# Batch 0 of a linear-attention and MLP kernel: nine tokens to a partition, and 64x64 products in place of 128x128 ones

## The chip, the core and the metric

The kernel runs on one core of a Trainium2 chip. The metric is the device time of one execution in microseconds (us). The engines of the core are TensorE (PE in the profile, its weight loads PEld), VectorE (DVE), ScalarE (ACT), GpSimd (POOL) and SyncE (SP). Each works through its own queue in program order and waits there for semaphores. GpSimd, SyncE and ScalarE also issue DMA transfers.

## What is computed

Eight batches of linear attention with eight heads, 576 tokens and a head size of 64 are followed by a two-layer MLP with a residual. Cut to what matters:

```python
q_s = softmax(q, axis=-1)                 # over the 64 columns of a head
k_s = softmax(k, axis=2)                  # over the 576 tokens
kv  = einsum('bhsd,bhse->bhde', k_s, v)   # 64x64 per head
x   = einsum('bhsd,bhde->bhse', q_s, kv)  # then heads side by side: (8, 576, 512)
xn  = (x - mean(x)) / sqrt(var(x) + 1e-6) * g_ln
out = x + maximum(xn @ w_ch1, 0) @ w_ch2  # 512 -> 2048 -> 512
```

All inputs and the output are float32. The kernel computes in bfloat16 with float32 accumulation.

## The kernel before

The tokens are worked off in chunks: chunk c from 0 to 7 is the first 512 tokens of batch c, as four tiles of 128 tokens, and chunk 8 holds the last 64 tokens of all eight batches. While TensorE runs the MLP of one chunk, the attention of the next chunks is done beside it. `run` (line 849) walks the list of the MLP's products and puts each side job ahead of the product at which its due number is reached. The program order on every engine is thus written out by hand.

Batch 0 has no earlier MLP to lie beside. It is done in `first_batch` (lines 957 to 1053), and this is what the change rewrites. Its steps are:

- **Loads.** SP issues q's first two tiles (line 978) and then k in four pieces of two heads (line 980). POOL waits for q by copying a few of its elements (`gate`, line 1004), and then issues v in three pieces (line 1006, four, two and two heads, cast to bfloat16 by the DMA), q's last two tiles (line 970), the first 512 columns of w1 in two pieces (line 1013, rows 0 to 255 and 256 to 511), the rest of w1, w2, and the loads of batches 1 and 2 (`load_behind`, line 1067).
- **Layout.** k and v of batch 0 have six tokens of a head in one partition (`T0 = 6`), so that 576 tokens fill 96 partitions.
- **Warm products.** `warm` (line 863) runs products of zeros on TensorE while the data is on its way.
- **q.** `exp_qt` (ScalarE), `norm_q` (VectorE: sum, reciprocal, product) and `eq_pT` (transposes on TensorE, copied out) for tiles 0 and 1.
- **k and v.** For each pair of heads j: `exp_k0` (line 293), the column sums `z0_mm` (line 306, six products with a column of ones), and `kv0_mm` (line 321, six products of 128 columns). The 128x128 result of a pair has the two heads' 64x64 blocks on its diagonal. VectorE takes it out times the reciprocal sum and times a block mask `diag` (line 322), straight into `kv_sb`, and sums each row. ScalarE (line 327) or, for the last pair, VectorE (line 331) spreads the row sum, times -1/512, over 128 columns (`mbc`).
- **x, transposed.** `xT_mm` (line 342) forms x less its mean for tiles 0 and 1, already transposed: one product with `kv_sb` and products with `mbc`, which subtract the mean. `xT_out` takes it out times g.
- **q, tiles 2 and 3.** `exp_qt` and `eq_pT` for them lie among the x products; their x is made later by `q0_rest` (lines 940 and 414), beside the first MLP products.

The first layer of chunk 0 (`mm1_part`, line 520) starts with w1's rows 0 to 255 for four output blocks, and then goes to rows 256 to 511. The two calls of `q0_rest` lie among the first eight of its products. Batch 1's k-v products (`kv_pairs`, line 371) come near the end of chunk 0; they need v of batch 1 (cast by VectorE, line 146) and the exponentials of k's last 64 tokens (line 198). Later batches form x by 64x64 products in two banks (`po_block`, line 403).

Of the kernel before, what the change touches and what calls it, by code (L numbers as in the profile page):

```python
# [20 lines left out]
def kernel(  # L21
# [34 lines left out]
    T0 = 6  # L56
    P0 = S // T0
# [18 lines left out]
    junk = const.tile([P, 256], BF16)  # L76
# [211 lines left out]

    def exp_k0(j):
        hs = slice(2 * j, 2 * j + 2)  # L290
        if j == 0:
            eks[0] = raw.tile([P, T0, H, D], BF16, tag="kt", name="ek0", bufs=1)
        nc.scalar.activation(
            eks[0][0:P0, :, hs, :].rearrange("p t h d -> p h t d"), raws[0][0][0:P0, hs], AF.Exp
        )

    def k0_mm(j, t):
        hs = slice(2 * j, 2 * j + 2)
        return eks[0][0:P0, t, hs, :], raws["v0"][0:P0, hs, t, :], P

    def z0_mm(j):

        if j == 0:
            kvbox["z0"] = mm_ps.tile([P, NP], FP32, tag="m", name="z0")
        for t in range(T0):
            nc.tensor.matmul(
                kvbox["z0"][:, j : j + 1], k0_mm(j, t)[0], ones[0:P0],
                start=(j == 0 and t == 0), stop=(t == T0 - 1), skip_group_check=True,
            )
# [6 lines left out]
    def kv0_mm(j):  # L316
        pool, tag = (att_ps, "a") if j < 2 else (mm_ps, "m")
        pkv = pool.tile([P, P], FP32, tag=tag, name="pkv")
        for t in range(T0):
            lhsT, rhs, w = k0_mm(j, t)  # L320
            nc.tensor.matmul(pkv[:, 0:w], lhsT, rhs, start=(t == 0), stop=(t == T0 - 1))
        nc.vector.scalar_tensor_tensor(
            kv_sb[:, 0, j, :], in0=pkv, scalar=kvbox["rz"][:, j : j + 1], in1=diag,
            op0=ALU.mult, op1=ALU.mult, accum_out=kvbox["sum"][:, j : j + 1],
        )
        if j < NP - 1:
            nc.scalar.activation(
                mbc[:, j], ones_w, AF.Copy, scale=kvbox["sum"][:, j : j + 1]
            )
        else:  # L330
            nc.vector.tensor_scalar_mul(
                out=mbc[:, j], in0=ones_w, scalar1=kvbox["sum"][:, j : j + 1]
            )

    def xT_mm(j, kh):
# [3 lines left out]
        ops = [(kv_sb[:, 0, j, :], j % 2)] if j // 2 == kh else []  # L339
        ops += [(mbc[:, j], i) for i in range(2)]  # L340
        for n, (lhsT, i) in enumerate(ops):
            nc.tensor.matmul(
                pobox["T", kh][:, i], lhsT, eqTs[0][:, 0:2, j, :],
                start=(j == 0 and n == 0), stop=(j == NP - 1 and n >= len(ops) - 2),
                skip_group_check=True,
            )

    def xT_out(i):
        dst, src = xnTs[0][:, 0:2, i, :], pobox["T", i // 2][:, i % 2]
        if i < 2:  # L350
# [3 lines left out]

    halves = (slice(0, 64), slice(64, P))
# [507 lines left out]
    def warm(n, width=256):  # L863

        w = mm_ps.tile([P, 512], FP32, tag="m", name="warm")
        for _ in range(n):
            nc.tensor.matmul(w[:, 0:width], junk[:, 0:P], junk[:, 0:width], start=True, stop=True)
# [83 lines left out]
    def g_columns():  # L951
        gcp = mm_ps.tile([P, KO1], FP32, tag="m", name="gcp")
        nc.tensor.matmul(gcp, raws["g"], ident_f, start=True, stop=True)
        nc.vector.tensor_copy(out=g_one, in_=gcp)
        nc.vector.tensor_scalar_mul(out=g_col, in0=gcp, scalar1=1.0 / DM)

    def first_batch():
# [3 lines left out]
            mlp.tile([P, H, T0, D], FP32, tag="hT", name="kt0", bufs=1), None,  # L961
# [3 lines left out]
        v0 = mlp.tile([P, H, T0, D], BF16, tag="hs", name="v0", bufs=1)  # L965
# [9 lines left out]
        def src0(x, h0, hn):  # L975
            return x[0, h0 : h0 + hn].rearrange("h (p t) d -> p h (t d)", t=T0)

        load_q0(0, 2, nc.sync)
        for h0 in range(0, H, 2):
            nc.sync.dma_start(  # L980
                k0[0:P0, h0 : h0 + 2].rearrange("p h t d -> p h (t d)"), src0(k, h0, 2)
            )
# [10 lines left out]
        nc.vector.memset(ones_w, -1.0 / DM)  # L993
        nc.vector.memset(diag, 0.0)
        for ps in halves:
            nc.vector.memset(diag[ps, ps], 1.0)
        nc.vector.memset(kv_sb[:, 1:B], 0.0)
# [7 lines left out]
        for h0, hn in ((0, 4), (4, 2), (6, 2)):  # L1005
            nc.gpsimd.dma_start(  # L1006
                v0[0:P0, h0 : h0 + hn].rearrange("p h t d -> p h (t d)"), src0(v, h0, hn)
            )
# [12 lines left out]
        warm(34)  # L1021
# [28 lines left out]
        eq_pT(0, 3, nc.vector)  # L1050
        xT_mm(3, 1)
        xT_out(2)
        xT_out(3)

# [136 lines left out]
```

## Time and profile before

| | us |
|---|---|
| median of 3 runs | 263.01 |
| lowest and highest | 262.71 and 263.16 |
| the profiled execution | 262.68 |
| its span, first to last instruction | 260.9 |
| TensorE busy in the span | 254.9 (98%) |
| VectorE busy | 223.3 (86%) |
| ScalarE busy | 177.8 (68%) |
| GpSimd busy | 103.4 (40%) |
| last k exponential of batch 0 ends | 10.29 |
| first k-v product of batch 0 starts | 10.56 |
| first MLP product starts | 15.24 |
| second piece of w1 lands | 17.04 |

The last four rows are positions in the span, counted from its start. A line of a timeline has the start in us, the duration in us, the engine, the line of the kernel, the operation, what it writes and reads, shapes, and the count of instructions merged in it; a bracket at the end gives the idle time of the engine just before and what ended it. The durations of merged products include the time that the last one takes to come out of the array (about 0.2 us), so the starts, not the durations, tell the rate. The granted TensorE clock is 0.997 over the span.

### The profile page before, as it was taken

The numbers are of one execution on the slowest core, as the hardware profiler recorded it, in microseconds if no ns is written. First come the engines' busy times: TensorE is split into PE (matmuls) and PEld (weight loads), VectorE is DVE, ScalarE is ACT, GpSimd is POOL, SyncE is SP. The second block draws the span as 40 slices with busy tenths as digits, with TensorE's granted clock in tenths as the row PEclk, the third lists the DMA queues.
The fourth block names the chain that finished last, engine by engine and source line by source line (L and its number), as shares of the span: only waits on it lengthen the run. The fifth ranks groups of instructions, "written<-read, shape, count | busy, mean of one in ns | idle before, by whom it ended". The sixth has DMA issues, their size and how long they took to land.

```text
span 260.9 us, 7328 instructions
## 1 busy us (share of the span) xinstructions
PE 254.9 (98%) x2904; PEld 218.6 (84%) x2907; DVE 223.3 (86%) x542; ACT 177.8 (68%) x348; POOL 103.4 (40%) x160
## 2 busy tenths in 40 slices
PE   8999999999999999999999999999999999999993
PEld 5889855788888888888888888888888888888883
DVE  6778996989998998899889988998899889957873
ACT  4657790997987785788578857885788386638400
POOL 3953138230199409800890098009100910190000
PEclk9999999999999999999999999999999999999998
DMA  6999999998899996998889968998902630322014
GB/s 190 255 206 206 352 221 274 275 213 273 151 121 314 272 110 139 293 242 88 119 287 259 95 133 290 244 96 166 276 1 45 140 143 4 72 72 101 3 40 121
DMA packets 82618, 45.04 MB, mean 173 GB/s; under 512 B 58196, under 2 KB 79192, under 8 KB 82584
## 3 DMA queue, kind: packets, MB, share of 16 engines
q0 software_dynamic: 32464, 21.76, 44.9%
q1 hardware_dynamic: 49488, 22.29, 37.0%
q10 hardware_dynamic: 632, 0.53, 0.7%
q8 instruction: 22, 0.36, 0.6%
q14 instruction: 12, 0.10, 0.1%
HBM read 36.70 MB, written 9.44 MB: 177 GB/s over the span
## 4 chain that ended last, share of the span: by engine, by line
PE 92%; DMA 4%; POOL 2%; issue 0%; DVE 0%
PE ba L604 21%; PE bx L762 20%; PE bb L762 10%; PE ph L520 8%; PE bb L604 6%; PE be L604 5%; PE bc L604 5%; PE pc L556 5%; PE bc L762 5%; DMA w_raw<-in_moe_w_ch_dram 3%; PE pkv L371 2%; DMA qt<-in_q_dram 2%; PE po L403 2%; PE ptr L928 1%; PE po L414 1%; POOL v L1006 1%
## 5 line engine op out<-in xcount | busy, mean ns | idle before, releaser
L604 PEld LDWEIGHTS <-hs 128*128 128x128 bf16 x512 | 49.6, 98 | 6.0
L269 POOL TENSOR_TENSOR tq<-xnT 128x256 bf16<-128x256 bf16 x30 | 20.1, 671 | 85.5 <-PE bc L604 59.9
L762 PEld LDWEIGHTS <-w_raw 128*128 128x128 bf16 x480 | 46.6, 98 | 5.8 <-DVE bb L793 0.2
L604 PEld LDWEIGHTS <-hT 128*128 128x128 bf16 x392 | 37.6, 98 | 4.2
L762 PEld LDWEIGHTS <-w1g 128*128 128x128 bf16 x360 | 34.7, 98 | 4.3 <-issue 0.2
L762 PE MATMUL bx<-tq,w_raw 128*128 128x256 bf16 x240 | 31.5, 273 | 0.0
L604 PE MATMUL ba<-w_q,hs 128*128 128x256 bf16 x256 | 30.6, 273 | 0.0
L786 ACT COPY bc<-bx 128x512 f32<-128x512 f32 x30 | 16.7, 594 | 19.1 <-PE bx L762 19.1
L427 ACT ACTIVATE scrap<-x,mv 128x512 bf16<-128x512 bf16 x32 | 23.1, 723 | 4.6 <-DVE mv L457 4.4
L793 DVE TENSOR_TENSOR bb<-bx,s 128x512 f32<-128x512 f32 x30 | 19.5, 694 | 7.8 <-ACT s L790 5.1
L804 ACT ACTIVATE hT<-bb 128x512 bf16<-128x512 f32 x30 | 16.3, 594 | 9.5 <-PE bb L762 9.5
L804 ACT ACTIVATE hT<-bc 128x512 bf16<-128x512 f32 x30 | 16.4, 595 | 8.5 <-PE bc L762 8.5
L796 DVE TENSOR_TENSOR hT<-bx,s 128x512 bf16<-128x512 f32 x30 | 19.3, 684 | 2.9 <-PE bx L762 2.7
L587 DVE TENSOR_TENSOR hs<-hT 128x1024 bf16<-128x1024 bf16 x32 | 21.3, 672 | 0.5 <-ACT hT L804 0.5
L229 DVE TENSOR_REDUCE zq<-eq 128x16 f32<-128x1024 bf16 (+1 forms) x20 | 20.7, 1048 | 0.5 <-ACT eq L220 0.5
L269 POOL TENSOR_TENSOR tq<-xnT,tq 128x256 bf16<-128x256 bf16 x30 | 20.0, 669 | 1.1
L449 DVE SCALAR_TENSOR_TENSOR x<-po,rq 128x256 bf16<-128x256 f32 x48 | 17.5, 420 | 1.6 <-PE po L403 1.6
L790 ACT COPY s<-bb 128x512 f32<-128x512 f32 x30 | 16.5, 620 | 0.0
L804 ACT ACTIVATE hT<-bx 128x512 bf16<-128x512 f32 x30 | 16.4, 608 | 0.0
L762 PE MATMUL bx<-xnT,w1g 128*128 128x256 bf16 x120 | 16.2, 273 | 0.0
L762 PE MATMUL bx<-tq,w1g 128*128 128x256 bf16 x120 | 15.9, 272 | 0.0
L762 PE MATMUL bc<-xnT,w1g 128*128 128x256 bf16 x120 | 15.8, 273 | 0.0
(157 smaller groups left out, 539.3 us busy)
## 6 DMA issues: line engine op xcount, KB each, us to landing
out_dram<-ot POOLq DMA_DIRECT2D x30, 256.0 KB, 5.0
kt<-in_k_dram SPq DMA_DIRECT2D x5, 1024.0 KB, 12.5
qt<-in_q_dram SPq DMA_DIRECT2D x4, 1024.0 KB, 8.7
qt<-in_q_dram POOLq DMA_DIRECT2D x2, 1024.0 KB, 12.9
kt<-in_k_dram POOLq DMA_DIRECT2D x2, 1024.0 KB, 14.7
vm<-in_v_dram POOLq DMA_DIRECT2D x16, 128.0 KB, 12.5
qt<-in_q_dram SPq DMA_DIRECT2D x3, 512.0 KB, 7.2
w_raw<-in_moe_w_ch_dram POOLq DMA_DIRECT2D x3, 512.0 KB, 10.8
```

Of the source, the lines that this page charges most:

```text
L229: nc.vector.reduce_sum(eqs[c][1][:, ts], eqs[c][0][:, ts], axis=AX.X)
L269: nc.gpsimd.tensor_tensor(out=dst[:, t], in0=x[:, t], in1=y[:, t], op=ALU.subtract)
L427: nc.scalar.activation(scrap, x[:, t], AF.Square, bias=mv[:, t, 0:1], scale=-float(DM), accum_out=mv[:, t, 1:2],)
L449: nc.vector.scalar_tensor_tensor(x[:, t].rearrange("p (i two d) -> p i two d", two=2, d=D)[:, :, half], in0=pobox[c, t][half], scalar=1.0, ...
L520: nc.tensor.matmul(ph[:, m % 2, at : at + tn], (w1g if c else w1_sb)[:, ko, m * P : (m + 1) * P], xnTs[c][:, t0 : t0 + tn, ko, :], start=( ...
L587: nc.vector.tensor_tensor(out=dst, in0=x, in1=y, op=op)
L604: nc.tensor.matmul(hbox[bank][:, t, cs], lhsT, rhs[:, cs], start=first and (own or t == 0) and k == 0, stop=k == KH - 1, skip_group_check= ...
L762: nc.tensor.matmul(dst[:, q], lhsT, rhs, start=first and q == 0 and ko == 0, stop=ko == 1, skip_group_check=True)
L786: nc.scalar.copy(at[g, "c"], at[g, "x"])
L793: nc.vector.tensor_tensor(out=at[g, "b"], in0=at[g, "x"], in1=at[g, "s"], op=ALU.add)
L796: nc.vector.tensor_tensor(out=h_out(g, 1, 1), in0=at[g, "x"], in1=at[g, "s"], op=ALU.add)
L804: nc.scalar.activation(h_out(g, odd, half), at[g, name], AF.Relu)
```

## The change

Five things change, nearly all in `first_batch` and its helpers:

1. `T0` goes from 6 to 9. A pair of heads then fills all 128 partitions, one head in each half (64 partitions of nine tokens). k still comes in four loads, and v now in four loads of one pair each in place of three.
2. The k-v and z products become 64x64 quarter products, one for each half: 18 per pair in place of six, both halves into one bank. The result of a pair is 128 partitions by 64 columns without the zero blocks, and goes to a new tile `kvc`. The block mask and its memsets go; `kv_sb` is filled from `kvc` by ScalarE copies (`kv0_copy`).
3. The row sum is scaled into one column (`kvm`) by VectorE, and the mean products read that column spread by a step of zero. `mbc` goes. The products of x with k-v become two quarter products per pair.
4. The order is rewritten: x is accumulated for both halves of its columns as each pair comes, warm products between the transposes go from 11 of 256 columns to two of 512, the leading 34 of 256 become 17 of 512, g's columns are copied by ScalarE, and `xT_out` and the last transposes are dealt differently to VectorE and ScalarE. The exponential of q's fourth tile moves behind `xT_out(1)`.
5. In `load_behind`, k's last 64 tokens are loaded ahead of v for batches 1 and 2.

```diff
-    T0 = 6
-    P0 = S // T0
+    T0 = 9
...
-    ones_w = const.tile([P, P], BF16)
-    diag = const.tile([P, P], FP32)
-    mbc = const.tile([P, NP, P], BF16)
+    ones_f = const.tile([P, D], FP32)
+    kvc = const.tile([P, NP, D], BF16)
+    kvm = const.tile([P, NP], BF16)
...
+            eks[0] = raw.tile([P, NP, T0, D], BF16, tag="kt", name="ek0", bufs=1)
+        nc.scalar.activation(eks[0][:, j], raws[0][0][:, j], AF.Exp)
...
         for t in range(T0):
-            nc.tensor.matmul(
-                kvbox["z0"][:, j : j + 1], k0_mm(j, t)[0], ones[0:P0],
-                start=(j == 0 and t == 0), stop=(t == T0 - 1), skip_group_check=True,
-            )
+            for ps in halves:
+                nc.tensor.matmul(
+                    kvbox["z0"][ps, j : j + 1], eks[0][ps, j, t], ones[ps],
+                    start=(j == 0 and t == 0), stop=(t == T0 - 1), skip_group_check=True,
+                )
...
     def kv0_mm(j):
-        pool, tag = (att_ps, "a") if j < 2 else (mm_ps, "m")
-        pkv = pool.tile([P, P], FP32, tag=tag, name="pkv")
+        pkv = att_ps.tile([P, D], FP32, tag="a", name="pkv")
         for t in range(T0):
-            lhsT, rhs, w = k0_mm(j, t)
-            nc.tensor.matmul(pkv[:, 0:w], lhsT, rhs, start=(t == 0), stop=(t == T0 - 1))
+            for ps in halves:
+                nc.tensor.matmul(
+                    pkv[ps], eks[0][ps, j, t], raws["v0"][ps, j, t],
+                    start=(t == 0), stop=(t == T0 - 1), skip_group_check=True,
+                )
         nc.vector.scalar_tensor_tensor(
-            kv_sb[:, 0, j, :], in0=pkv, scalar=kvbox["rz"][:, j : j + 1], in1=diag,
+            kvc[:, j], in0=pkv, scalar=kvbox["rz"][:, j : j + 1], in1=ones_f,
             op0=ALU.mult, op1=ALU.mult, accum_out=kvbox["sum"][:, j : j + 1],
         )
...
+        nc.vector.tensor_scalar_mul(
+            out=kvm[:, j : j + 1], in0=kvbox["sum"][:, j : j + 1], scalar1=-1.0 / DM
+        )
+
+    def kv0_copy(js):
+        for ps in halves:
+            nc.scalar.copy(kv_sb[ps, 0, js, ps], kvc[ps, js])
+
+    def xT_mean(j, kh):
...
+        for i in range(2):
             nc.tensor.matmul(
-                pobox["T", kh][:, i], lhsT, eqTs[0][:, 0:2, j, :],
-                start=(j == 0 and n == 0), stop=(j == NP - 1 and n >= len(ops) - 2),
+                pobox["T", kh][:, i], kvm[:, j : j + 1].to_broadcast([P, P]),
+                eqTs[0][:, 0:2, j, :], start=(j == 0 and i == 0), stop=(j == NP - 1),
                 skip_group_check=True,
             )
+    def xT_kv(j):
+        kh, i = divmod(j, 2)
+        for ps in halves:
+            nc.tensor.matmul(
+                pobox["T", kh][ps, i], kvc[ps, j], eqTs[0][ps, 0:2, j, :],
+                start=False, stop=False, skip_group_check=True,
+            )
...
     def xT_out(i):
-        if i < 2:
+        if i % 2 == 0:
             nc.vector.tensor_scalar_mul(out=dst, in0=src, scalar1=g_one[:, i : i + 1])
...
+    def g_copies():
+        nc.scalar.copy(g_one, raws["gcp"])
+        nc.scalar.activation(g_col, raws["gcp"], AF.Copy, scale=1.0 / DM)
...
+        def src0(x, j):
+            return x[0, 2 * j : 2 * j + 2].rearrange("two (s t) d -> (two s) (t d)", t=T0)
...
+        for j in range(NP):
+            nc.gpsimd.dma_start(v0[:, j].rearrange("p t d -> p (t d)"), src0(v, j))
...
-        nc.vector.memset(kv_sb[:, 1:B], 0.0)
+        nc.vector.memset(ones_f, 1.0)
+        nc.vector.memset(kv_sb, 0.0)
...
-        warm(34)
+        warm(17)
         for t in range(2):
             exp_qt(0, t)
             norm_q(0, t)
         eq_pT(0, 0, nc.vector)
-        warm(11)
-        eq_pT(0, 1, nc.vector)
         for j in range(NP):
             exp_k0(j)
-            z0_mm(j)
-            if j == NP - 2:
-                g_columns()
+        z0_mm(0)
+        g_columns()
+        z0_mm(1)
+        warm(2)
+        eq_pT(0, 1, nc.vector)
+        z0_mm(2)
+        z0_mm(3)
+        g_copies()
         recip_z()
         kv0_mm(0)
         kv0_mm(1)
+        kv0_copy(slice(0, 2))
+        def xT(j):
+            xT_mean(j, 0)
+            xT_mean(j, 1)
+            xT_kv(j)
+        xT(0)
         kv0_mm(2)
-        xT_mm(0, 0)
+        xT(1)
         kv0_mm(3)
         exp_qt(0, 2)
-        exp_qt(0, 3)
-        xT_mm(1, 0)
-        xT_mm(2, 0)
-        xT_mm(0, 1)
-        xT_mm(3, 0)
+        xT(2)
+        kv0_copy(slice(2, 4))
+        xT_mean(3, 0)
         xT_out(0)
         xT_out(1)
-        eq_pT(0, 2, nc.scalar)
-        xT_mm(1, 1)
-        xT_mm(2, 1)
-        eq_pT(0, 3, nc.vector)
-        xT_mm(3, 1)
+        eq_pT(0, 2, nc.vector)
+        exp_qt(0, 3)
+        xT_mean(3, 1)
+        xT_kv(3)
         xT_out(2)
         xT_out(3)
+        eq_pT(0, 3, nc.vector)
...
             if which == 1:
+                load_krem(nc.gpsimd, b)
                 load_v(b)
-                load_krem(nc.gpsimd, b)
```

More of the change, by code (lines that the diff above doesn't have):

```diff
@@ L861, in run, with warm @@
             fn()
-    def warm(n, width=256):
-        w = mm_ps.tile([P, 512], FP32, tag="m", name="warm")
+    def warm(n):
+        w = mm_ps.tile([P, 4, P], FP32, tag="m", name="warm")
         for _ in range(n):
-            nc.tensor.matmul(w[:, 0:width], junk[:, 0:P], junk[:, 0:width], start=True, stop=True)
+            nc.tensor.matmul(w, junk, junk[:, 0:4].to_broadcast([P, 4, P]), start=True, stop=True)
     def prep_fast(b):
@@ L951, in g_columns @@
     def g_columns():
[L952 to L955, printed above, removed]
+        raws["gcp"] = mm_ps.tile([P, KO1], FP32, tag="m", name="gcp")
+        nc.tensor.matmul(raws["gcp"], raws["g"], ident_f, start=True, stop=True)
+    def g_copies():
+        nc.scalar.copy(g_one, raws["gcp"])
+        nc.scalar.activation(g_col, raws["gcp"], AF.Copy, scale=1.0 / DM)
     def first_batch():
@@ L964, in first_batch @@
         k0, _, q0 = raws[0]
[L965 removed]
+        v0 = mlp.tile([P, NP, T0, D], BF16, tag="hs", name="v0", bufs=1)
         raws["v0"] = v0
```

42 lines of the change are left out of this document (5 added, 37 removed).

## The prediction

> **What bounds the kernel now.** I read the windows by stage first. From 45 us to 250 us TensorE is busy without a gap (40.00 of 40.00 us in the line below), and its steps stand in one written order; so whatever comes late or early before 45 us is handed on to the end in full.
>
> ```profile
> 60.00:100.00 40.00, 40.00 (x460) 35.04 (x458) 37.52 (x89) 32.36 (x65) 19.49 (x28) 1.00 1.12 214
> ```
>
> The columns are: stretch, PE, PEld, DVE, ACT and POOL busy, granted clock, DMA share, GB/s. Next the chain that ended last, in order of time: it comes over the second piece of w1 (line 1013, rows 256 to 511 of 512 columns), which lands at 17.04, and from there it is TensorE.
>
> ```profile
> 9.86 7.18 DMA w_raw<-in_moe_w_ch_dram
> 17.04 0.05 issue
> 17.09 0.61 PE ph L520 x4
> ```
>
> Then the timeline of the prologue. The group at 17.09 is the first that needs w1's second piece.
>
> ```profile
> 7.46 0.40 PE L928 MATMUL ptr<-ident,eq 128*128 128x128 bf16 x4
> 10.56 1.25 PE L321 MATMUL pkv<-v,ek 96*128 96x128 bf16 x18
> 11.09 0.35 DVE L322 SCALAR_TENSOR_TENSOR kv_sb<-pkv,rzk,diag 128x128 bf16<-128x128 f32 x1 [0.22 <-PE pkv L321]
> 13.70 0.39 PE L342 MATMUL pxT<-eqT,mbc 128*128 128x256 bf16 x2 [0.26 <-DVE mbc L331]
> 15.24 0.60 PE L520 MATMUL ph<-xnT,w_raw 128*128 128x256 bf16 x4
> 16.55 0.38 PE L414 MATMUL po<-kv_sb,eqT 128*128 128x128 bf16 x4
> 17.09 0.61 PE L520 MATMUL ph<-xnT,w_raw 128*128 128x256 bf16 x4 [0.16 <-DMA w_raw<-in_moe_w_ch_dram]
> ```
>
> The last four products before 17.09 start at 16.55 and follow each other by 0.055, so TensorE alone would have gone on at 16.77. That is 1.53 us after the MLP's first product (15.24), and only 0.32 us ahead of w1. Two paths are level here, loads and TensorE, and the change works on both: the time moves by the later of the two, less 17.09.
>
> **The loads.** In the one-us windows, 4 to 5 moves q (128 partitions) at 390 GB/s and 5 to 8 moves k (96 partitions) at 267 to 269:
>
> ```profile
> 4.00:5.00 1.00, 1.00 (x7) 0.71 (x5) 0.88 (x1) 0.00 (x0) 0.00 (x0) 1.00 1.12 390
> 7.00:8.00 1.00, 1.00 (x13) 0.80 (x11) 1.00 (x2) 0.75 (x2) 1.00 (x2) 1.00 1.09 268
> ```
>
> k is 1.18 MB: 4.4 us at 268, 3.0 at 390. If 128 partitions bring k to q's rate, all that stands behind it (DMA share above 1 in every window from 3 us) comes 1.4 us sooner, and w1's second piece lands at 15.6. Against that POOL issues four v loads for three. The three took 2.13 us, and those of 192 rows 0.65 to 0.67; a fourth puts w1's issue 0.5 to 0.67 later. If landing followed issue alone that is 17.7 at worst. Issue ends near 10.6 now, and the bytes ahead of it move until about 12.6, so I take 15.8. The exponential of a k pair, 0.84 us for 768 columns and 0.575 for q's 512, is 0.64 for 576. The last now ends at 10.29; it would end near 8.9, or 10.06 if k lands as now (9.42).
>
> **TensorE's price of a quarter product.** No row has two 64x64 products side by side. The nearest are the pair products of later batches (128x64, two side by side) and the x products (64x64, four side by side):
>
> ```profile
> 56.71 1.04 PE L762 MATMUL bb<-tq,w_raw 128*128 128x256 bf16 x8
> 57.68 0.32 PE L371 MATMUL pkv<-vm,ek 128*64 128x65 bf16 x8
> ...
> 58.30 0.20 PE L371 MATMUL pkv<-vr,ekr 128*64 128x65 bf16 x2
> 58.44 1.05 PE L762 MATMUL bx<-tq,w_raw 128*128 128x256 bf16 x8
> ```
>
> ```profile
> 91.05 0.49 PE L604 MATMUL ba<-w_sb,hT 128*128 128x256 bf16 x3
> 91.47 0.74 PE L403 MATMUL po<-kv_sb,eqT 64*64 64x64 bf16 x64
> 92.14 0.83 PE L604 MATMUL bb<-w_q,hs 128*128 128x256 bf16 x6
> ```
>
> Forty take 57.68 to 58.30, 16 ns each; 64 take 0.74 less the 0.19 of the last one, 8.7 ns each. I take 16, since two lie side by side in the change as well, for z0's one-column products too (bounds 8.7 and, one after the other, 32). Both blocks also show the price of changing over: full products follow each other by 0.109, so the line 371 block could have begun at 57.59 and began at 57.68 (0.09 in); its last starts at 58.30 and the next full one at 58.44 (0.12 out). Line 403 gives 0.09 and 0.11. The first line 371 block, at 42.22, was left in 0.34. I take 0.09 in and 0.12 out; 0.34 is the upper end, and nothing the lower.
>
> **The sum, up to the first pair product.** The transposes at 7.46 wait for VectorE as now and take 0.22: 7.68. z0(0): 0.09 + 18 x 0.016 + 0.12 = 0.50. g_columns: 0.24 (its two pieces stood 0.12 apart). z0(1): 0.50. warm(2): two of 512 columns, by the 0.216 spacing of line 556's, 0.43. That is 9.35, past the 9.02 at which the second transposes could go (norm_q ends at 8.96), so 0.33 us of that wait's cover is overdrawn. Transposes 0.22, into quarters 0.09, z0(2) and z0(3) 0.58: T = 10.24 for the first k-v product, against 10.56. v's first pair, the first of four, should have landed (the four-head load now lands near 10.5). The 34 warm products become 17 of twice the width: nothing. The 11 removed took 1.2 us, spent waiting for norm_q anyway.
>
> **From T to the MLP.** Now 15.24 - 10.56 = 4.68. After: the first VectorE take-out at T + 0.48 (18 x 0.016, the 0.17 that lay between last product and 11.09, a little for the handover). 64 columns for 128 save 0.07 of 0.35; its accumulator read and the one-column multiply (0.14 on line 1124) put kvm(0) at +0.46, so mean(0) starts at T + 1.00. It was ScalarE's 0.39 before. Four mean products 0.44 (1.44). A round of quarters, xT_kv(0) and kv0(2), is 0.09 + 0.12 + 0.29 + 0.12 = 0.62 (2.06). Mean(1) 0.44, round 0.62 (3.12). Mean(2) 0.44, xT_kv(2) with its changes 0.33 (3.89). kvm(3) is there at 3.70. The two of xT_mean(3,0) end at 4.27. Now the new wait: ScalarE's queue holds xT_out(1) and behind it exp_qt(0,3), where both late exponentials stood before any x copy. 0.42 for xT_out(1) (half of 0.84, line 353) and 0.575 for the exponential, with handovers: 5.32. TensorE stands at eq_pT(0,3) for it, and behind that the whole MLP, which needs nothing of it yet. Transposes 0.22: first MLP product at T + 5.58 = 15.82, 0.58 later than now. Plus the 1.53: **17.35 against 17.09, 0.26 us slower**, with w1 (15.8) no longer the last.
>
> **What costs nothing.** VectorE's memsets: kv_sb for eight batches for seven adds 0.22, without ones_w and diag 0.62 goes, ones_f adds about 0.1; all of it ends before the q exponential that the first reduction waits for (5.67). Without that cover it would be a gain of 0.3. g's two copies on ScalarE (0.4) fall between the k exponentials and kv0_copy; kv0_copy itself, two of at most 0.39 twice, ends at T + 4.3, level with xT_out(1): no cover left there. k's remainder ahead of v for batches 1 and 2: 128 KB in front of v, 0.4 to 0.6 us of queue; v's casts now end at 40.72, the pair products start at 42.22, and the line 198 exponential that they waited for comes sooner: 0 to -0.05.
>
> **Own time.** The profiled execution took 262.68 (span 260.9 and 1.8 around it), 0.33 under the median 263.01; the sum gives 262.94 there and 263.3 beside the median.
>
> **Rivals.** *Loads decide and quarters are cheaper: faster.* z0 at 8.7 ns takes 0.52 off T, and if the three changes in and out between mean(0) and mean(3,0) hide, 0.63 more: TensorE is ready at 16.2, w1 at 15.8 lets it, 0.9 us gained: 262.1. For: T's path has slack nowhere else. Against: both blocks above pay 0.2 each time. *Changing back costs 0.34, as at 42.22: slower.* Five of these lie on the path (z0(0), z0(1), three rounds): 5 x 0.22 = 1.1, together 1.36: 264.4. It decides from 0.17 us per change. Against: 0.11 to 0.12 at 58 and 92 us. *Quarters one after the other: slower.* At 32 ns T moves to 11.3, kv0(0), (2), (3) add 0.9 and the three xT_kv 0.3: ready at 19.6, 265.6. For: every row of 64x64 products writes its two row halves to two banks (line 402's bank), while here both halves share one; no row shows that. *The loads go no faster:* k's last exponential at 10.06, z0(3) behind it, T = 10.4, ready at 17.5, 263.4.
>
> The Trainium skill (TensorEngine Tiling (Array Packing), Gotcha 1: PSUM Pressure) says that different row tiles cannot write one PSUM bank at the same time; by that rule the third rival would hold, and line 403's rows, with two banks, can't speak to it.
>
> **How the numbers follow.** Forecast 0.30, faster rival 0.29, changing back 0.21, one after the other 0.10, loads no faster 0.10. A run tells about 0.2% (0.53 us) from no change. Of the forecast 0.24 lies within that, 0.045 above; of the loads rival 0.065 within; of the faster rival 0.22 is beyond it; of changing back 0.18, of the serial one all. Together faster 0.24, same 0.40, slower 0.36. The forecast's own range is 262.7 to 263.8; for 8 in 10 it goes from 262.0 (leaving out a quarter of the faster rival) to 264.4 (leaving out the serial one and a little more).
>
> **What would show it.** w1's second load at about 15.8 and no DMA wait at the line 520 group; ScalarE's last k exponential at 8.9; quarter products 16 ns apart with 0.2 per change; a TensorE gap of about half a us ending at the exponential of q's fourth tile; first MLP product near 15.8. I am wrong if that gap is missing, if T lies outside 9.7 to 10.6, or if a wait appears after 20 us that isn't there now.

## The result, and the profile after

| | before | after |
|---|---|---|
| median, us (22 runs each, side by side) | 263.04 | 264.19 |
| lowest and highest | 262.13 and 264.95 | 263.62 and 266.18 |
| ratio of the times, 95% interval | | 1.0048 (1.0033 to 1.0064) |

The change makes the kernel **slower by 1.15 us**. That is inside the stated 8-in-10 range (262.0 to 264.4), but outside the forecast's own range (262.7 to 263.8, about 263.3) and beyond the 0.2% that count as no change. The ratio here and below is not the quotient of the two medians; the two measures differ by up to 0.3%.

The profiled execution of the changed kernel took 265.6 us, 1.4 above its median. The same kernel was profiled once more (run r1, below) and took 264.24 with a span of 262.5. That one stands for the usual execution, so the timelines are read from it, and the first profile serves for the loads and for what goes wrong on top.

The windows by stage of the changed kernel's first profile (columns as in the prediction):

```profile
6.00:7.00 1.00, 0.66 (x4) 0.10 (x1) 0.93 (x3) 1.00 (x3) 1.00 (x3) 1.00 1.04 389
...
9.00:10.00 1.00, 1.00 (x44) 0.81 (x43) 0.51 (x2) 0.00 (x0) 1.00 (x3) 1.00 1.16 165
...
13.00:14.00 1.00, 1.00 (x23) 0.60 (x18) 0.45 (x3) 0.52 (x1) 0.80 (x2) 1.00 1.00 150
...
15.00:16.00 1.00, 0.01 (x2) 0.00 (x0) 0.66 (x2) 1.00 (x3) 0.65 (x1) 1.00 1.23 196
```

and two windows of the kernel before:

```profile
9.00:10.00 1.00, 1.00 (x25) 0.96 (x24) 0.72 (x2) 0.76 (x2) 1.00 (x3) 1.00 1.31 201
...
13.00:14.00 1.00, 0.74 (x8) 0.43 (x7) 0.60 (x3) 0.88 (x2) 1.00 (x2) 1.00 1.21 198
```

k now moves at 389 GB/s instead of 268, as forecast. But the loads behind it are slower than they were: v's window from 9 to 10 shows 165 GB/s, where the kernel before shows 201, and q and w1 from 13 to 14 show 150 where it shows 198. The DMA share stays at 1 or above (1.16 and 1.00, before 1.31 and 1.21), so the loads are slower without the DMA engines going idle. From 15 to 16 TensorE stands still (0.01 us busy).

The timeline of r1, the changed kernel's usual execution, from its first k-v product to the long run of first-layer products:

```profile
10.01 0.73 PE L315 MATMUL pkv<-v,ek 64*64 64x64 bf16 x36
...
11.05 0.61 PE L336 MATMUL pxT<-eqT,kvm 128*128 128x256 bf16 x4 [0.30 <-DVE kvm L323]
...
13.92 0.39 PE L336 MATMUL pxT<-eqT,kvm 128*128 128x256 bf16 x2
...
14.43 0.48 DVE L354 TENSOR_SCALAR xnT<-pxT,g_one 128x256 bf16<-128x256 f32 x1 [0.68 <-PE pxT L336]
...
14.94 0.47 ACT L356 ACTIVATE xnT<-pxT,g_one 128x256 bf16<-128x256 f32 x1 [0.74 <-DVE xnT L354]
...
15.16 0.47 DVE L354 TENSOR_SCALAR xnT<-pxT,g_one 128x256 bf16<-128x256 f32 x1
...
15.31 0.62 ACT L219 ACTIVATE eq<-qt 128x512 bf16<-128x512 f32 x1
...
15.99 0.40 PE L929 MATMUL ptr<-ident,eq 128*128 128x128 bf16 x4 [1.01 <-ACT eq L219]
...
16.62 0.61 PE L521 MATMUL ph<-xnT,w_raw 128*128 128x256 bf16 x4 [0.23 <-DMA w_raw<-in_moe_w_ch_dram]
...
18.15 0.60 PE L521 MATMUL ph<-xnT,w_raw 128*128 128x256 bf16 x4
...
19.02 0.40 PE L929 MATMUL ptr<-ident,xn 128*128 128x128 bf16 x4 [0.27 <-DVE xn L476]
```

Read from the top: the quarter products and the x products stand where the forecast put them, counted from the first k-v product. Then VectorE's copy of x (`xT_out(0)`, line 354) runs first, ScalarE's (`xT_out(1)`, line 356) waits for it, the exponential of q's fourth tile comes behind that, and TensorE waits 1.01 us for it at the transposes. Its next wait is for w1's first piece, and the one after that (19.02) is for VectorE: the normalized x of q's third tile.

The chain that ended last in r1, from w1's issue on:

```profile
9.09 7.48 DMA w_raw<-in_moe_w_ch_dram
16.57 0.05 issue
16.62 0.61 PE ph L521 x4
...
18.40 0.57 DVE xn L476
...
19.02 0.41 PE ptr L929 x4
...
20.86 0.48 DVE xn L476
...
21.38 0.40 PE ptr L929 x4
21.78 11.37 PE ph L521 x112
```

In the chain of the kernel before, the same line "PE ph x112", a run of 112 products without a gap, stood at 20.10: here it comes 1.68 us later. The four landmarks below follow the loss through the span (starts in us, from the timelines; the "long run" is the group of line 521, before 520, from which TensorE goes on without a wait):

| | before | after, r1 | later by |
|---|---|---|---|
| first MLP product | 15.24 | 16.62 | 1.38 |
| group that needed w1's second piece | 17.09 | 18.15 | 1.06 |
| long run of first-layer products | 19.93 | 21.62 | 1.69 |
| k-v products of batch 1 | 42.22 | 43.91 | 1.69 |
| k-v products of batch 2 | 57.68 | 59.36 | 1.68 |
| span | 260.9 | 262.5 | 1.6 |

So in the usual execution all of the loss is there by 21.6 us, and next to nothing is won or lost after it. (Of these two executions the one before was 0.36 under its median of this comparison; hence 1.6 here and 1.15 between the medians.) The first profile of the changed kernel lost more, after 40 us. In its timeline VectorE casts batch 1's v:

```profile
42.19 0.53 DVE L145 COPY vm<-vt 128x1024 bf16<-128x1024 bf16 x1 [1.86 <-DMA vt<-in_v_dram]
...
46.72 0.38 PE L415 MATMUL po<-kv_sb,eqT 128*128 128x128 bf16 x4 [0.47 <-DVE kv_sb L380]
```

The cast waits 1.86 us for the load and is 3.1 us later than before (39.04); the x products of batch 1 then wait 0.47 for VectorE. The chain of this execution runs over that load, not over w1: the late loads are a second cause that stands close behind the first. Waits of TensorE after 20 us that the kernel before doesn't have (this one, and 0.52 us for VectorE at 60.33) are one of the prediction's own signs of being wrong; r1 shows none.

### The profile page after: what moved, and what is told of

It is laid out like the page before. It is cut to its first block, busy times and chain, and to the rows that moved or that the text cites. A ratio compares the mean times of both kernels' runs of the same rounds, so it can differ in the third digit from the quotient of the medians.

```text
span 263.8 us, 7480 instructions
## 1 busy us (share of the span) xinstructions
PE 255.2 (97%) x2981; PEld 215.6 (82%) x2981; DVE 223.8 (85%) x541; ACT 176.0 (67%) x350; POOL 103.2 (39%) x161
## 4 chain that ended last, share of the span: by engine, by line
PE 76%; DMA 13%; POOL 3%; DVE 3%; ACT 2%; issue 1%
PE ba L605 21%; PE bx L763 20%; PE bb L763 10%; DMA vt<-in_v_dram 6%; DMA w_sb<-in_moe_w_ch_dram 6%; PE bb L605 6%; PE be L605 5%; PE bc L605 5%; PE bc L763 5%; PE pkv L372 2%; DMA qt<-in_q_dram 2%; PE po L404 2%; DVE w_q L571 1%; POOL v L1004 1%; POOL w_raw L98 1%
## 5 line engine op out<-in xcount | busy, mean ns | idle before, releaser
L268 POOL TENSOR_TENSOR tq<-xnT 128x256 bf16<-128x256 bf16 x30 | 20.1, 672 | 81.7 <-PE bc L605 45.7
L268 POOL TENSOR_TENSOR tq<-xnT,tq 128x256 bf16<-128x256 bf16 x30 | 20.1, 671 | 1.1
L763 PE MATMUL bb<-tq,w_raw 128*128 128x256 bf16 x120 | 15.7, 273 | 0.5 <-DVE hT L530 0.5
```

The lines of the kernel that those rows point to most:

```text
L268: nc.gpsimd.tensor_tensor(out=dst[:, t], in0=x[:, t], in1=y[:, t], op=ALU.subtract)
L763: nc.tensor.matmul(dst[:, q], lhsT, rhs, start=first and q == 0 and ko == 0, stop=ko == 1, skip_group_check=True)
```

## The experiments

All times are medians; each is compared with runs of the kernel before made beside it (263.01 beside r1 to r4, 263.19 beside r5 to r7, 262.7 beside r8 to r10, 263.43 beside r11 and r12).

### r1: the changed kernel again

No edit.

> The changed kernel unaltered, to see how much of its profile repeats. Order theory (ScalarE's queue, q's fourth exponential behind the x copy, makes TensorE late): about 264.2, first MLP product near 16.4 with a TensorE gap of about 1 us before the last transposes, in every execution. Load theory (w1's first piece lands late because the loads ahead of it move slower): w1's first piece again lands after 16 us and TensorE waits for it. If the profiled execution of before, 265.6, was a late one for its loads, the span here is near 262.4 and the wait for v of batch 1 at 42 to 44 us is smaller.

264.48 us (12 runs), ratio 1.0047 (1.0025 to 1.0069): the result again, with the profile shown above.

### r2: the exponential ahead of the copies

```diff
     def xT_out(i):
-        if i % 2 == 0:
+        if i < 2:
             nc.vector.tensor_scalar_mul(out=dst, in0=src, scalar1=g_one[:, i : i + 1])
...
         kv0_copy(slice(2, 4))
+        exp_qt(0, 3)
         xT_mean(3, 0)
         xT_out(0)
         xT_out(1)
-        eq_pT(0, 2, nc.vector)
-        exp_qt(0, 3)
+        eq_pT(0, 2, nc.scalar)
```

> The changed kernel with q's fourth exponential ahead of the x copies on ScalarE and both first x copies on VectorE, as the kernel before has them. Order theory: the last transposes go 0.6 to 0.8 us sooner (15.2 for 16.0) and the time falls by 0.5 to 0.8, to about 263.5. Load theory: TensorE then stands at its first MLP product for w1's first piece until 16 to 16.5, and the time falls by less than 0.3.

264.21 us (12 runs), ratio 1.0056 (1.0029 to 1.0084): no better than the changed kernel beside it (264.48, ratio 1.0047). The timeline of r2 shows both halves of that:

```profile
15.93 0.61 PE L521 MATMUL ph<-xnT,w_raw 128*128 128x256 bf16 x4 [0.27 <-DMA w_raw<-in_moe_w_ch_dram]
...
18.36 0.40 PE L929 MATMUL ptr<-ident,xn 128*128 128x128 bf16 x4 [0.29 <-DVE xn L476]
...
40.95 0.43 DVE L145 COPY vm<-vt 128x1024 bf16<-128x1024 bf16 x1 [1.32 <-DMA vt<-in_v_dram]
...
42.21 0.65 DVE L145 COPY vm<-vt 128x1024 bf16<-128x1024 bf16 x1 [0.83 <-DMA vt<-in_v_dram]
...
58.78 0.60 PE L763 MATMUL bb<-tq,w_raw 128*128 128x256 bf16 x4 [0.34 <-DVE hT L530]
```

The first MLP product comes 0.69 us sooner than in r1, and the k-v products of batch 1 still 0.68 sooner (43.23). But VectorE now waits 1.32 and 0.83 us for batch 1's v, the x products come 0.55 sooner only (45.35), and TensorE waits for VectorE's work at 58.78: the k-v products of batch 2 start at 59.31, against 59.36 in r1. So the order does cost TensorE what the prediction said it would, and more. Giving it back gains nothing in the end: in this timeline the late loads take all of it by 59 us.

### r3 and r4: k's remainder and v, in the old and the new order

r3 is the changed kernel with step 5 of the change undone; r4 is the kernel before with step 5 alone (the same two lines the other way round).

```diff
             if which == 1:
-                load_krem(nc.gpsimd, b)
                 load_v(b)
+                load_krem(nc.gpsimd, b)
```

> The changed kernel with k's remainder behind v again for batches 1 and 2. If the later v of batch 1 costs time (its casts wait at 42 to 44 us, TensorE then waits 0.5 us for k-v): 0.3 to 0.5 faster than the changed kernel, about 263.8. If the swap is free, as the prediction had it: 264.2 within 0.2. If it paid: slower by 0.3 or more, with a wait for the exponentials of k's remainder ahead of the k-v products.

> The kernel before with only the swap of k's remainder and v. Free, as the prediction had it: 263.0 within 0.2. If the later v costs: 263.3 to 263.6, with VectorE's wait for v before its casts longer than the 0.9 us of now and TensorE waiting at the k-v products of batch 1.

r3: 264.94 us (6 runs), ratio 1.0071 (1.0045 to 1.0098), 0.46 more than the changed kernel beside it. r4: 262.56 us (12 runs), ratio 0.9984 (0.9962 to 1.0007), 0.45 less than before, which the interval doesn't settle; nor is r3 settled against the changed kernel, with 6 runs and an interval that overlaps that one's (1.0025 to 1.0069). So step 5 shows no cost; it seems to gain some 0.45 us in either kernel, where the forecast had 0 to 0.05. The other four steps alone cost 1.93 (264.94 less 263.01). In r3's timeline the place is seen:

```profile
59.56 0.60 PE L763 MATMUL bb<-tq,w_raw 128*128 128x256 bf16 x4 [0.53 <-DVE hT L530]
```

TensorE waits there for VectorE, where r1 has no wait, and the k-v products of batch 2 start at 60.09 instead of 59.36.

r4's profiled execution was its longest (264.34), and shows something of TensorE:

```profile
10.85 1.29 PE L321 MATMUL pkv<-v,ek 96*128 96x128 bf16 x18 [0.53 <-DMA v<-in_v_dram]
...
13.49 1.91 PE L342 MATMUL pxT<-eqT,mbc 128*128 128x256 bf16 x8
```

Eight products take 1.91 us, about 0.21 apart, where the kernel before has them 0.109 apart; the granted clock reads 0.61 from 12 to 13 and 0.50 from 13 to 15. Half a us of waiting ahead of the k-v products came shortly before some 3 us at half rate. The wait alone isn't shown to be the reason: r1 waits 1.01 us at 15.99 and r11 (below) 1.14 us at 13.21, and the granted clock of both stays at 1.00 there.

### r5 and r6: v in shorter rows

The first theory of the late loads was the length of v's rows: 1152 bytes written per row now, 768 before. r5 writes each row as three of 384 bytes; r6 is r5 with r2's order.

```diff
-        v0 = mlp.tile([P, NP, T0, D], BF16, tag="hs", name="v0", bufs=1)
+        v0 = mlp.tile([P, NP, 3, 4, D], BF16, tag="hs", name="v0", bufs=1)
...
-            nc.gpsimd.dma_start(v0[:, j].rearrange("p t d -> p (t d)"), src0(v, j))
+            nc.gpsimd.dma_start(
+                v0[:, j, :, 0:3].rearrange("p g t d -> p g (t d)"),
+                src0(v, j).rearrange("p (g x) -> p g x", g=3),
+            )
```

> The changed kernel with each partition's nine tokens of v cast into three rows of three tokens with a gap between them in the tile (384 B written at a time for 1152). Row theory (rows of 1152 written bytes leave each DMA engine waiting between packets, 107 ns each and no overlap): v then moves at 200 GB/s or more as in the kernel before, is in by about 10.8 us for 11.4 to 12.1, w1's first piece lands by 15.3, and the time falls by 0.3 to 0.8. Cast theory (casting into all 128 partitions is what is slow, or the stalls come from elsewhere): v still needs 4.4 us or more and w1's first piece lands after 16; 264.2 within 0.3.

> The same three-token rows with q's fourth exponential ahead of the x copies. If loads were the second limit that hid the order's gain: first MLP product at about 15.5 for 16.6, no DMA wait before it, and 0.8 to 1.3 faster than the changed kernel, 262.9 to 263.4. If the loads stay late: as the order alone, 264.2.

r5: 266.13 us (6 runs), ratio 1.0103 (1.0069 to 1.0136). r6: 265.13 us (7 runs), 1.0081 (1.0049 to 1.0113). The theory falls: the first MLP product comes at 18.08 and 18.79, where r1 has 16.62. (In r6 q's fourth tile itself was late, with one packet of 3.35 us.) The chain of r5:

```profile
5.49 3.16 POOL v L1004 x4
8.65 1.79 POOL qt L973 x2
10.44 7.59 DMA w_raw<-in_moe_w_ch_dram
18.03 0.05 issue
18.08 0.61 PE ph L521 x4
```

Three times as many rows take POOL 3.16 us to issue instead of 2.23, w1 is issued at 10.44 instead of 9.09, and then takes as long as ever (7.59; r1 7.48).

### What the DMA records show, and r7 to r10

The single packets in the records of the DMA tell more than the windows. Counted for v and w1 up to 20 us:

| | v's rows, bytes written | median packet of v, ns | packets of v / w1 over 200 ns | w1 packets begun by 20.1 us |
|---|---|---|---|---|
| before | 768 | 79 | 0 / 0 | 1483 |
| after | 1152 | 107 | 7 / 19 | 1374 |
| r1 | 1152 | 107 | 12 / 28 | 1331 |
| r4 (before, step 5 alone) | 768 | 79 | 1 / 1 | 1496 |
| r5 (three short rows) | 384 | 51 | 22 / 18 | 1057 |
| r7 (v by SyncE, not cast; k's rows counted with v's) | 2304 | 95 | 2 / 0 | 1521 |

In the changed kernel the usual packet is in order, but a few dozen take 0.2 to 1.7 us each, where v's and w1's usually take 0.1. The kernel before has none of these. The load of q's tiles 2 and 3 is the same in both kernels, and it slows down as well: none of its 128 packets took over 200 ns before (median 194.5), 76 and 79 of them in the first profile and in r1 (median 240 and 279). Four runs looked for what brings the stalls.

```diff
# r7: v as float32 by SyncE behind k, cast by four ScalarE copies
+        for j in range(NP):
+            nc.sync.dma_start(v0f[:, j], src0(v, j))
...
-        for j in range(NP):
-            nc.gpsimd.dma_start(v0[:, j].rearrange("p t d -> p (t d)"), src0(v, j))
...
+        for j in range(NP):
+            nc.scalar.copy(
+                raws["v0"][:, j].rearrange("p t d -> p (t d)"), raws["v0f"][:, j]
+            )
# r8: rows of 1152 bytes, 1280 bytes apart
-        v0 = mlp.tile([P, NP, T0, D], BF16, tag="hs", name="v0", bufs=1)
+        v0 = mlp.tile([P, NP, T0 + 1, D], BF16, tag="hs", name="v0", bufs=1)
# r9: every ninth token in a load of its own, then rows of 1024 bytes
+        nc.gpsimd.dma_start(
+            v0[:, :, 8],
+            v[0].rearrange("(j two) (s t) d -> (two s) j t d", two=2, t=T0)[:, :, 8],
+        )
         for j in range(NP):
-            nc.gpsimd.dma_start(v0[:, j].rearrange("p t d -> p (t d)"), src0(v, j))
+            nc.gpsimd.dma_start(
+                v0[:, j, 0:8].rearrange("p t d -> p (t d)"), src0(v, j)[:, 0 : 8 * D]
+            )
# r10: r7, POOL's loads only once k is in, and both late exponentials ahead of the x copies (dealt as in r2)
-        nc.gpsimd.tensor_copy(out=gate, in_=q0[:, 1, 0, 0:4])
+        nc.gpsimd.tensor_copy(out=gate, in_=k0[:, NP - 1, 0, 0:4])
...
         exp_qt(0, 2)
+        exp_qt(0, 3)
         xT(2)
```

> The changed kernel with v loaded as float32 by SyncE behind k and cast by ScalarE in four instructions, to see the same rows moved without a cast. Row theory: they are slow without a cast too, under 340 GB/s. Cast theory: k's rows of the same length moved at 390 GB/s, so v does too, is in by 10.5, and w1's first piece lands near 15. The time itself suffers from ScalarE's casts (some 2.7 us ahead of the k-v copies and the q exponentials): 264 to 266, not of interest.

> The changed kernel with v's written rows of 1152 B set 1280 B apart, so that each starts at a multiple of 256 B. If the start of the written rows is what holds the DMA engines up: no packets over 200 ns in v and the first w1 loads, w1's first piece by 15.3, and 0.3 to 0.8 faster. If it is the length, or the cast of such rows whatever they start at: as the changed kernel, 264.2 within 0.3.

> The same 1280 B apart, with the ninth tokens of all pairs in a first load of 128 B rows and tokens 0 to 7 in four loads of 1024 B rows, the row length of w1. If the length of 1152 is what holds the engines up: the 1024 B packets near 98 ns as w1's, none over 200, v in by 11.2, and the time 0.2 to 0.6 faster in spite of one load more. If any cast of v there does it: stalls as before, 264.2 to 264.6.

> v uncast by SyncE and cast by ScalarE as in the run before, POOL's queue held until k's last pair has landed so that v goes first, and both late q exponentials ahead of the x copies. If late loads and ScalarE's order are together the whole loss: first MLP product at 15.4 to 15.7, w1's second piece before 16, batch 2's k-v products at or before 58 us, and 262.6 to 263.2, the time of the kernel before. If the quarter products themselves cost it: still over 263.8.

| | median us (runs) | ratio (95%) | first MLP product | long run |
|---|---|---|---|---|
| r7 | 264.95 (11) | 1.0075 (1.0044 to 1.0105) | 16.77 | 21.43 |
| r8 | 264.86 (10) | 1.0070 (1.0040 to 1.0099) | 16.71 | 21.72 |
| r9 | 264.9 (10) | 1.0070 (1.0037 to 1.0102) | 17.20 | 22.23 |
| r10 | 265.5 (9) | 1.0074 (1.0036 to 1.0111) | 16.62 | 21.30 |

r8 and r9 have the same stalled packets (14 of v and 9 of w1 in r8, 51 together in r9): neither where a row starts nor its length of 1152 bytes brings them. r7 is all but free of them, and w1's first piece lands at 14.7, where r1 has it at 16.57. Its windows and timeline:

```profile
8.00:9.00 1.00, 1.00 (x39) 0.95 (x39) 0.93 (x4) 0.90 (x3) 1.00 (x2) 1.00 1.06 401
9.00:10.00 1.00, 1.00 (x26) 0.66 (x26) 0.56 (x3) 0.91 (x5) 1.00 (x2) 1.00 1.08 406
```

```profile
12.57 0.67 ACT L1036 CAST v<-v 128x576 bf16<-128x576 f32 x1 [1.27 <-DMA v<-in_v_dram]
...
16.54 0.40 PE L929 MATMUL ptr<-ident,eq 128*128 128x128 bf16 x4 [1.01 <-ACT eq L219]
```

The loads run at 400 GB/s, yet the kernel is no faster: v now writes twice as many bytes, beside POOL's q and w1, so its last pair lands at 12.55, and ScalarE must cast it ahead of the exponential that TensorE waits for. The stalls are gone, but their cure costs as much on the TensorE path, so r7 doesn't part the two causes. r10 let v through first (landed by 10.94), but then the stalls were back (54 packets of w1), although nothing of v was cast by the DMA any more, and the exponential of q's fourth tile waited for its load:

```profile
14.83 0.63 ACT L219 ACTIVATE eq<-qt 128x512 bf16<-128x512 f32 x1 [1.84 <-DMA qt<-in_q_dram]
...
16.62 0.61 PE L521 MATMUL ph<-xnT,w_raw 128*128 128x256 bf16 x4 [0.71 <-DMA w_raw<-in_moe_w_ch_dram]
```

So the cast of v isn't what brings the stalls. r7's loads with r2's order, but without r10's wait on k, were not tried.

### r11 and r12: TensorE's instruction count

The records also show transfers of 16 KB that carry TensorE's instructions. The first came at 14.58 in the kernel before and at 11.2 and 11.8 in the changed one, in the midst of v and w1; TensorE had started 123, 139 and 149 products by then. r11 gives the kernel before as many more (the warm products halved in width and doubled in number); r12 gives the changed kernel fewer. r12 leaves out the column sums over eight of the nine tokens of a partition.

```diff
# r11, from the kernel before
-        warm(34)
+        warm(68, 128)
...
-        warm(11)
+        warm(22, 128)
# r12, from the changed kernel
-        for t in range(T0):
+        for t in (T0 - 1,):
...
-        warm(2)
+        warm(4)
...
         z0_mm(3)
+        warm(3)
```

> The kernel before with its 34 and 11 warm products of 256 columns as 68 and 22 of 128: as many columns, 45 products and 45 weight loads more ahead of the first data, loads and all else unaltered. The instruction transfer of 16 KB that stands in the DMA records at 14.6 us, when TensorE has done some 120 products, should then come at 10 to 11 us, as in the changed kernel. Instruction theory (that transfer, coming early between v and w1, holds up a DMA engine and with it w1 and all that follows): w1's first piece lands 1 to 1.7 us later than 14.8, packets over 200 ns appear in q and w1, and the time rises by 0.4 to 1.2. Against it: packets and landings as in the kernel before, and 262.7 within 0.3.

> The changed kernel with 8 of its 72 z products (it leaves out the column sums over eight of a partition's nine tokens; the values of batch 0 are then wrong in scale) and five more warm products of 512 columns in their place, so that TensorE's time up to the first k-v product stays and 59 products and as many weight loads go. Instruction theory: the 16 KB transfer comes near 13 us and later than v and most of q, there are fewer packets over 200 ns, w1's first piece lands before 15.8, and the time falls by 0.3 to 0.7. Against it: v's and w1's packets stall as before the edit, w1's first piece after 16, and 264.2 within 0.3.

r11: 263.49 us (12 runs), ratio 1.0006 (0.9990 to 1.0021). The transfer came at 11.13, and the profiled execution waits for v:

```profile
13.21 0.49 PE L321 MATMUL pkv<-v,ek 96*128 96x128 bf16 x6 [1.14 <-DMA v<-in_v_dram]
```

w1's first piece came at 15.7, one us later than in the profile before (14.7), but only 4 of w1's packets and none of v's stood over 200 ns, and the median didn't move. r12: 264.46 us (12 runs), ratio 1.0045 (1.0026 to 1.0064), as the changed kernel. Its one profiled execution ran TensorE at a fraction of its rate (span 876.7 us), so only its loads are read. With TensorE that slow, the instruction transfer came at 28.64, long after v and w1, and the first quarter products at 15.64; 13 packets of v and 30 of w1 stalled all the same, 35 of these 43 before that product. So neither the instruction transfer nor the quarter products are what stalls the packets, though the transfer delays a load.

How it does so shows in the landings. The record has sixteen for each of these loads, and a load is in with the last of them. In the kernel before, fifteen landings of w1's second piece came by 16.06 and the last at 17.04: the landing from which the prediction starts was one late part. In r11 fifteen landings of v's last load came by 11.70 and the last at 13.16, and in w1's two pieces the last stands 1.2 us behind the others too (15.70 and 16.98). In both kernels the late part appears within one load of the start of the transfer (14.58 and 11.13), and so it does in r3 (13.40; w1's first piece 16.45, the other fifteen by 15.28). I read it as the transfer's doing; no run took the transfer alone away. In r1 three landings of w1's first piece are late (16.15, 16.21 and 16.57, the other thirteen by 15.34).

## Why the prediction was right and wrong

The prediction put the group of the prologue that counted before (17.09) at 17.35, +0.26 us, and let it be handed on from there. The direction came out, the size didn't: the medians lie 1.15 apart, and r1 has +1.69 at the long run. The 1.43 between 1.69 and 0.26, term by term (r1's timeline; T is the start of its first k-v product):

| term | forecast | r1 | off by |
|---|---|---|---|
| T | 10.24 | 10.01 | -0.23 |
| T to the last transposes | 5.36 | 5.98 | +0.62 |
| last transposes to the first MLP product | 0.22 | 0.63 | +0.41 |
| from there to the group at 17.09 before | 1.53 | 1.53 | 0 |
| that group to the next (0.67 before) | 0.67 | 1.10 | +0.43 |
| the next to the long run (2.17 before) | 2.17 | 2.37 | +0.20 |
| sum | | | +1.43 |

**Right: the price of a quarter product and of changing over.** 36 products take 0.73 us, less 0.19 for the last one 15.4 ns each (forecast 16; one after the other would have been 32). T itself came 0.23 sooner, of which 0.18 is no merit of the forecast: q landed sooner, and the first transposes started at 7.28 instead of 7.46. mean(0), (1), (2) and (3,0) start at T + 1.04, 2.09, 3.14 and 3.91 in r1, against 1.00, 2.06, 3.12 and 3.89. That takes out three rivals: quarters at 8.7 ns, changes at 0.34, and quarters one after the other. The last was the rule of the Trainium skill (TensorEngine Tiling (Array Packing), Gotcha 1: PSUM Pressure) that different row tiles can't write one bank at the same time; here both halves write one bank, and the trace doesn't agree.

**Right: k's load.** k moves at 389 to 392 GB/s, its last piece lands 1.6 us sooner (7.85 in r1, 9.43 before; forecast 1.4), and its last exponential ends at 8.54 to 8.56 (forecast 8.9).

**Right by luck: that w1's second piece is no longer the last.** The group at 18.15 waits for no DMA. But the piece landed at 17.82, not at 15.8; had TensorE been ready at 17.35 as forecast, it would have stood for it. The measured time also lies nearest to that of the rival "changing back costs 0.34" (264.4), whose mechanism the rows above rule out.

**Right in place, short by half: the exponential behind the x copy.** The prediction said that TensorE would stand at the last transposes for q's fourth tile, for about half a us; it stands for 1.01. The step that was mis-sized is "0.42 for xT_out(1)", which let it start at T + 4.32, beside `xT_out(0)`. It started at T + 4.93, behind it: the bracket `[0.74 <-DVE xnT L354]` says that ScalarE sat idle for VectorE's copy. Both read one tile of PSUM and write one tile of x. The shared tile of x isn't the reason: VectorE's `xT_out(2)` writes the same one, out of the other PSUM tile, and starts at 15.16 while ScalarE's copy still runs (14.94 to 15.41). That leaves the shared PSUM tile; no run gave the two copies a tile each. In the kernel before, copies 0 and 1 were both VectorE's, so no row of it showed the wait. r2, which takes the exponential out from behind both, wins 0.69 us at the first MLP product.

**Wrong: "w1's second piece lands at 15.6 ... so I take 15.8", and all the loads behind k.** The first piece, which was to come well before, lands at 16.57 in r1 (14.7 before) and TensorE waits for it; the second piece comes at 17.82. The fear that a fourth v load would hold up w1's issue was wrong too: the four take POOL 2.23 us against 2.06 for three, and w1 is issued at 9.09, before it was 9.22. What failed is counting bytes at a steady rate. The 1.6 us that k had won were gone with v, whose last load landed at 11.97 (12.11 before). And the rate tells at best the middle of a load: half of the second piece's landings were in by 16.1 (15.6 before), but TensorE needs the last (17.82; 17.04 before). Packets stall. It costs 0.41 us here. I read the lateness of w2 and of batch 1's v as the same one carried on: in r2 it eats the 0.69 us between 43 and 59 us, and in the first profile of the changed kernel it adds to the loss. The two causes look level: r2, with the order mended alone, gains nothing. But no run had both mended, so their shares in the 1.15 us are not shown.

**Missed: what is late next behind w1.** The prediction took TensorE alone to set what follows 17.09. But q's tiles 2 and 3 go through VectorE (x, then its normalization, line 475 before and 476 after). Before, that result was ready at 17.37 and the transposes that read it came at 17.53. Without the wait for w1 they would have come at 17.21 (16.77 and 0.44 for the group), ahead of VectorE: the wait was its cover. With it gone TensorE stands 0.27 us for VectorE at 19.02. And VectorE itself is slower there. The timelines of r1 and of r10, both with their first MLP product at 16.62:

```profile
18.11 0.76 POOL L102 DMA_DIRECT2D w_sb<-in_moe_w_ch_dram  x1
...
18.40 0.56 DVE L476 TENSOR_SCALAR xn<-x,st 128x512 bf16<-128x512 bf16 x1
...
20.61 0.63 POOL L136 DMA_DIRECT2D ktr<-in_k_dram  x1 [1.74 <-DMA w_raw<-in_moe_w_ch_dram]
...
20.86 0.47 DVE L476 TENSOR_SCALAR xn<-x,st 128x512 bf16<-128x512 bf16 x1
```

```profile
18.40 0.35 DVE L476 TENSOR_SCALAR xn<-x,st 128x512 bf16<-128x512 bf16 x1
18.42 0.76 POOL L102 DMA_DIRECT2D w_sb<-in_moe_w_ch_dram  x1 [0.36 <-DMA w_raw<-in_moe_w_ch_dram]
...
20.65 0.35 DVE L476 TENSOR_SCALAR xn<-x,st 128x512 bf16<-128x512 bf16 x1
20.93 0.63 POOL L136 DMA_DIRECT2D ktr<-in_k_dram  x1 [1.75 <-DMA w_raw<-in_moe_w_ch_dram]
```

Where POOL began to issue a DMA shortly before, the normalization takes 0.56 and 0.47 us; where the normalization comes first, 0.35, as in the kernel before:

```profile
17.02 0.35 DVE L475 TENSOR_SCALAR xn<-x,st 128x512 bf16<-128x512 bf16 x1
...
17.32 0.76 POOL L103 DMA_DIRECT2D w_sb<-in_moe_w_ch_dram  x1 [1.14 <-DMA w_raw<-in_moe_w_ch_dram]
```

That is 0.33 of the 0.63 us, and r10's long run does start 0.32 sooner than r1's (21.30). The Trainium skill (SBUF — State Buffer, Who interferes with whom) has the rule: VectorE in a two-port mode and GpSimd, which writes the descriptors, share a pair of ports, and whoever starts first holds it. The traces agree only in part: the stretch (0.12 to 0.21 here) is less than POOL's whole issue (0.63 to 0.76), and in r11 a normalization that started at 17.77, 0.51 us into an issue of 0.76, still took 0.35. In all profiles the stretched ones started 0.18 to 0.31 us after POOL. No run moved POOL's issue alone, so that part is read from the timelines, not tested.

**Wrong: "k's remainder ahead of v ... 0 to -0.05".** r3 and r4 both put it near 0.45 us on the good side, neither settling it alone. Without it the forecast would have been further off.

**What stays open.** The stalled packets were in every profile in which k and v fill 128 partitions and POOL alone loads from some 10 us on (after, r1, r2, r3, r5, r6, r8, r9, r10, r12); there were two short ones in r7, where SyncE's queue moved beside POOL's until 11.5, and none to four in the three profiles with 96 partitions (before, r4, r11). Row length, row start, the cast of v, TensorE's instruction transfer and its quarter products are ruled out as the sole cause. What it is, these runs don't say. Nor is there a version that is shown to beat the kernel before; r4 is the nearest.

## What to carry to other kernels

When a wait is about to go, list every engine that was working under its cover, not only the next load: here VectorE's normalization was 0.16 us later than TensorE would have been without its wait. When the copies out of one PSUM tile are dealt to two engines, take them one after the other in the sum until a row shows them side by side. And a first load that gets faster is no proof that those behind it come sooner: take the time from issue to landing as the profile has it, ask whether one late part sets it, and check the last landing against the next deadline (here batch 1's v at 40 us) before counting a gain elsewhere.

## What the hardware showed unexpectedly

- Single packets of 0.2 to 1.7 us among GpSimd's loads of v and w1, whose median packets take 107 and 98 ns, a few dozen between 7 and 17 us; cause open.
- A load of 96 partitions moves 268 GB/s and one of 128 partitions 390 GB/s, both float32 on SyncE's queue.
- Two diagonal 64x64 products into one PSUM bank run side by side: 36 in 0.73 us, 15.4 ns apart. (By the 0.109 us of a 256-column product, 64 columns alone would take an estimated 27.)
- VectorE's 128x512 bfloat16 normalization takes 0.35 us alone and 0.46 to 0.66 when POOL began to issue a DMA 0.18 to 0.31 us before (r1, r2, r3, r5, r6, r8, r9, r11 and the first profile); 0.35 again when POOL began 0.51 before (r11).
- TensorE at half its granted clock for some 3 us, shortly after a wait of 0.53 us (r4's profile); longer waits in r1 and r11 left the clock at 1.00. Cause open.
- TensorE's instructions come by DMA 16 KB at a time, 0.9 to 1.3 us each; the first transfer starts when TensorE has begun 104 to 191 products, depending on the run, the second at 244 to 257 in all runs but r12 (203).
- A load is in with the last of sixteen landings, and a single one can stand 1 us and more behind the others (w1's second piece before: 17.04 against 16.06).
